# Three low bits of nine weight blocks taken from a byte on ScalarE; the order of the work searched anew

## The chip, the core and the metric

The kernel runs on one core of a Trainium2 chip. The metric is the device time of one execution, in microseconds (us); lower is better. The engines are TensorE (PE; its weight loads are shown apart as PEld), VectorE (DVE), ScalarE (ACT), GpSimd (POOL) and SyncE (SP), which issues nearly all DMAs.

## What is computed

Attention in which a query sees only the keys of its own cluster, followed by a feed-forward layer with a clipped square as its activation. Cut to what matters:

```python
# q, k, v: (4, 8, 768, 64) float32; centroids: (8, 16, 64)
q_assign = argmax(q_n . c_n); k_assign = argmax(k_n . c_n)      # normed rows
scores = where(q_assign == k_assign, q @ k.T / 8, -1e9)
attn = softmax(scores) @ v
x = attn laid out as (3072, 512)
h = x @ w_in                     # w_in: (512, 2048), w_out: (2048, 512)
g = where(h >= 1, h, where(h <= -1, 0, (h + 1)**2 / 4))
out = g @ w_out
```

The two weight matrices come in as float64. The kernel reads each weight as two 32-bit words, a low and a high one, and builds the float32 of it by shifting bits.

## The kernel before

The 3072 tokens are worked in twelve units u of 256 tokens, three to a batch entry. A unit has four pairs of heads, and a pair has four score tiles of 128 x 768. For each tile TensorE makes the scores into a two-bank PSUM buffer `pair` (`at_scores`), VectorE evicts them with their row minimum into `sS` (the instruction shown as CUSTOM_DVE_ANT_0, called an eviction below; evictions are counted from 1, so the 17th is the first of the second unit), ScalarE takes the exponential (`at_soft`), and TensorE multiplies with v (`at_av`). The first unit works in float32 and transposes its exponentials on TensorE; later units split each number into two float16 parts, which ScalarE and GpSimd make, and transpose by DMA. Then each unit goes through eight blocks f of 256 hidden columns (`ffn1`, `ffn2`).

Ahead of the first score tile stand the loads of q and k, their scaling and splitting, the labels (`labels`: products with the centroids and five VectorE passes that find the nearest one) and the mask rows made of the labels (`k_assign`, `q_pairs`). `v_bound` finds the largest v of a pair of heads (one VectorE reduction each, tile `v_am`).

Beside this the weights are prepared once, in sixteen blocks i = 2f + a (a is 0 for w_in, 1 for w_out), each of 1024 numbers on 128 partitions. A block is loaded with two DMAs (`w_load`) and then goes through `w_bits` (L1152): ScalarE takes the absolute value of the high words, scaled, into `t` (the buffers o, wk in the profile); VectorE shifts `t` left by three (L1170, the shift pass); TensorE sums columns of `t` to bound the weights (`w_sum`); VectorE ORs in the top three bits of the low words (the OR pass); and VectorE ORs in the sign while it writes the finished block to `w` (the sign pass). In the profile the shift pass is TENSOR_SCALAR 128x1024 and the other two are SCALAR_TENSOR_TENSOR 128x1024. `w_split` later makes the float16 parts.

What runs when is not the order of the code. Every operation goes to a `Recorder`, which holds the graph of what depends on what. `issue` runs a planner of its own forward and backward over it, `BASE` times, then shifts priorities by a list of numbers (`NUDGES`), each the seed of one change of priorities that `nudge` makes, and writes all instructions out in the order of the last forward pass. Each engine then takes its own instructions strictly in that order, and so does SP with the DMAs. Since all of them are written out by one helper, every row of the profile has line L376, and rows are told apart by their tiles.

Of the kernel before, what the change touches and what calls it, by code (L numbers as in the profile page):

```python
# [10 lines left out]
BF16 = mybir.dt.bfloat16  # L11
F32 = mybir.dt.float32
U32 = mybir.dt.uint32
AF = mybir.ActivationFunctionType
ALU = mybir.AluOpType
AX = mybir.AxisListType
# [26 lines left out]
FETCH = [128 * k - min(42, 4 + 9 * k) for k in range(1, 80)]  # L43

LOOK, MARGIN = 0.4, 4000
BASE = 21
NUDGES = (
# [29 lines left out]
)  # L77
TILED = 248

# [457 lines left out]
def tile_clustered_attention_moe(  # L537
# [38 lines left out]
    EARLY_SPLITS = 4  # L576
    WA, WR = -4, 2.6

    RAW = [3, 4, 5, 6, 7, 4, 5, 6, 0, 7, 6, 7, 0, 7, 0, None]
    rec = Recorder(tc)  # L580
    const = ctx.enter_context(tc.tile_pool(name="const", bufs=1))
# [195 lines left out]
    def k_scale(b, hp):  # L777
# [14 lines left out]

        ib = ar.bitcast(U32)
        rec.vector.tensor_scalar(
# [357 lines left out]
    def w_bits(a, f, part=None):  # L1152

        raw = WL.pop((a, f, part))
# [3 lines left out]
        t = WL[a, f][0][:, (part or 0) * 512 :][:, :n]  # L1158
        dst = w32[a][f][:, (part or 0) * 512 :][:, :n]
        tf = t.bitcast(F32)  # L1160
        if not w_wide:
# [5 lines left out]

        lo, hi = (raw.rearrange("p (f a) -> p f a", a=2)[:, :, x] for x in range(2))
        rec.scalar.activation(out=tf, in_=hi.bitcast(F32), func=AF.Abs, scale=2.0**-112)
        rec.vector.tensor_scalar(out=t, in0=t, scalar1=3, scalar2=None, op0=ALU.logical_shift_left)  # L1170
        w_sum(a, f, part)

# [2 lines left out]
            out=to, in0=lo, scalar=29, in1=t, op0=ALU.logical_shift_right, op1=ALU.bitwise_or  # L1175
        )
        rec.vector.scalar_tensor_tensor(
            out=dst, in0=hi, scalar=0x80000000, in1=to, op0=ALU.bitwise_and, op1=ALU.bitwise_or
# [192 lines left out]
    for i in range(2 * NF):  # L1371
        f, a = divmod(i, 2)
# [47 lines left out]
```

## Time and profile before

| | us |
|---|---|
| median of 3 runs | 852.74 (852.6 to 853.91) |
| the profiled execution | 851.57 |
| its span, from the first to the last instruction | 849.8 |
| PE busy | 808.7 (95%) |
| ACT busy | 657.6 (77%) |
| DVE busy | 633.3 (75%) |
| POOL busy | 529.5 (62%) |

The shares are means over the whole span. The kernel has a first part, in which loads, labels, float32 attention and weight preparation come together, and a long even part behind it, so the page's forty slices, and the busy time of each engine by stretch, say more than the means do. The rows themselves stand further below.

### The profile page before, as it was taken

How to read it: one execution, taken by the hardware profiler on the slowest of the kernel's cores; microseconds unless marked ns; L12 is line 12 of the kernel's file. 1: busy time of each engine (PE TensorE's matmuls, PEld its weight loads, DVE VectorE, ACT ScalarE, POOL GpSimd, SP SyncE). 2: the span in 40 equal slices, each digit the busy share in tenths (PEclk: the TensorE clock that was granted, in tenths of full speed). 3: DMA queues.
4: the chain of work that ended last, by engine and by line, in shares of the span. 5: the costliest groups of instructions: out<-in, count | busy, mean ns of one | idle time of the engine just before them, and what ended most of it. 6: DMA issues, size and time to landing. Idle time of an engine off the chain costs nothing.

```text
span 849.8 us, 18811 instructions
## 1 busy us (share of the span) xinstructions
PE 808.7 (95%) x7052; PEld 559.7 (66%) x7052; DVE 633.3 (75%) x1400; ACT 657.6 (77%) x1166; POOL 529.5 (62%) x510
## 2 busy tenths in 40 slices
PE   3686999999999999999999999999999999999998
PEld 2465776666766676766776767666676667677664
DVE  6999998999897768578888658677888766454322
ACT  6778999899987788788778688788778778676332
POOL 1121698978987568666767668657667668566222
PEclk9699999999999999999999999999999999999999
DMA  8967899979989779879989779889999788565100
GB/s 296 311 178 199 229 198 202 191 137 208 185 174 187 152 160 187 162 152 223 215 168 186 133 152 180 173 186 196 196 179 158 124 163 157 98 133 109 24 25 25
DMA packets 404763, 142.50 MB, mean 168 GB/s; under 512 B 372800, under 2 KB 396352, under 8 KB 404672
## 3 DMA queue, kind: packets, MB, share of 16 engines
q1 hardware_dynamic: 404672, 141.30, 82.0%
q8 instruction: 55, 0.90, 0.5%
q14 instruction: 36, 0.29, 0.1%
HBM read 40.40 MB, written 6.29 MB: 55 GB/s over the span
## 4 chain that ended last, share of the span: by engine, by line
PE 71%; DVE 7%; ACT 5%; issue 4%; POOL 3%; DMA 1%; POOLq 0%; DVEq 0%; ACTq 0%
PE pair L376 36%; PE banka L376 10%; PE banki L376 9%; PE bankh L376 9%; PE bankj L376 8%; DVE sS L376 2%; POOL hl L376 2%; DMA pT<-hl 1%; ACT hl L376 1%; ACT sS L376 1%; POOL w L376 1%; DVE r L376 1%; DVE w L376 1%; DVE bankh L376 1%; ACT w L376 1%
## 5 line engine op out<-in xcount | busy, mean ns | idle before, releaser
L376 POOL TENSOR_TENSOR hl<-sS,hl 128x768 f16<-128x768 f32 x176 | 297.6, 1694 | 113.5 <-ACT hl L376 96.9
L376 PE MATMUL pair<-w,g 128*128 128x512 f16 (+1 forms) x1120 | 277.3, 391 | 0.6 <-DVE w L376 0.6
L376 PEld LDWEIGHTS <-w 128*128 128x128 f16 x2112 | 204.8, 98 | 40.6 <-issue 1.6
L376 DVE CUSTOM_DVE_ANT_0 sS<-pair,zero,er 128x768 f32<-128x768 f32 x192 | 193.8, 1011 | 50.5 <-PE pair L376 41.2
L376 ACT ACTIVATE sS<-sS,sbi 128x768 f32<-128x768 f32 x192 | 179.1, 933 | 66.9 <-DVE sbi L376 61.7
L376 PEld LDWEIGHTS <-g 128*128 128x128 f16 x1056 | 101.6, 98 | 106.8 <-issue 1.2
L376 PE MATMUL pair<-kv,q 128*128 128x384 f16 x768 | 157.9, 329 | 6.9 <-DVE sbi L376 4.5
L376 ACT CAST hl<-sS 128x768 f16<-128x768 f32 x176 | 144.8, 826 | 7.3 <-DMA pT<-hl 5.4
L376 POOL TENSOR_TENSOR g<-r,g 128x512 f16<-128x512 f32 x80 | 95.4, 1192 | 75.5 <-ACT g L376 65.6
L376 PEld LDWEIGHTS <-q 128*128 128x128 f16 x992 | 78.3, 98 | 62.2 <-issue 18.5
L376 PE MATMUL banka<-pT,kv 128*64 128x256 f16 (+1 forms) x1680 | 104.8, 279 | 0.0
L376 PEld LDWEIGHTS <-kv 128*64 128x64 f16 (+1 forms) x1824 | 92.1, 108 | 5.5 <-DMA kv<-n 1.9
L376 ACT ACTIVATE r<-r,f_ra,f_rs 128x512 f32<-128x512 f32 x80 | 64.8, 810 | 38.3 <-DVE r L376 37.9
L376 POOL TENSOR_TENSOR qn<-qn,phi 128x256 f16<-128x256 f16 x48 | 32.7, 697 | 41.2 <-DVE phi L376 15.6
L376 PE MATMUL bankj<-x,w 128*128 128x256 f16 (+1 forms) x424 | 57.4, 289 | 0.0
L376 ACT CAST g<-r 128x512 f16<-128x512 f32 x80 | 48.7, 609 | 8.8 <-DVE r L376 5.5
L376 PE MATMUL bankh<-x,w 128*128 128x256 f16 (+1 forms) x376 | 47.2, 277 | 0.0
L376 PE MATMUL banki<-x,w 128*128 128x256 f16 (+1 forms) x288 | 39.9, 291 | 0.0
L376 PE MATMUL banki<-wk,w 128*128 128x256 f16 x312 | 37.0, 273 | 0.0
L376 ACT ACTIVATION_READ_ACCUMULATOR sS<-sS,sbi 128x1 f32 x192 | 36.0, 188 | 0.0
L376 DVE TENSOR_SCALAR r<-bankh,f_lo,f_hi 128x512 f32<-128x512 f32 x27 | 21.8, 808 | 18.2 <-PE bankh L376 16.3
L376 DVE TENSOR_SCALAR r<-banki,f_lo,f_hi 128x512 f32<-128x512 f32 x27 | 21.8, 808 | 15.9 <-PE banki L376 10.7
(262 smaller groups left out, 1108.5 us busy)
## 6 DMA issues: line engine op xcount, KB each, us to landing
w<-in_moe_w_out_dram SPq DMA_DIRECT2D x14, 512.0 KB, 6.0
kv<-in_k_dram SPq DMA_DIRECT2D x16, 384.0 KB, 3.9
q<-in_q_dram SPq DMA_DIRECT2D x12, 512.0 KB, 4.9
kv<-in_v_dram SPq DMA_DIRECT2D x16, 384.0 KB, 4.2
out_dram<-o SPq DMA_DIRECT2D x11, 512.0 KB, 3.4
w<-in_moe_w_in_dram SPq DMA_DIRECT2D x10, 512.0 KB, 5.3
word<-in_moe_w_in_dram SPq DMA_DIRECT2D x6, 512.0 KB, 4.8
o<-in_v_dram SPq DMA_DIRECT2D x8, 384.0 KB, 3.8
```

The lines of the kernel that those rows point to most:

```text
L376: fn(*args, **kw)
```

## The change

For the first nine blocks (i = 0 to 8) `w_bits` takes another way. The top byte of each low word is read as an unsigned byte, every eighth byte of the raw block. ScalarE computes byte/32 - 15.5/32 and writes it as an integer over the low word, which leaves the top three bits of the byte. VectorE then shifts `t` and ORs in these bits in one instruction, and the sign pass follows as before. So these blocks have two passes on ScalarE and two on VectorE, where there were one and three. `w_sum` now stands behind the pass that has the low bits in it. The other seven blocks stay as they were. `BASE` goes from 21 to 24, and the list of seeds is a new one.

```diff
+U8 = mybir.dt.uint8
...
-BASE = 21
+BASE = 24
 NUDGES = (
...
+    LO3 = range(9)
     RAW = [3, 4, 5, 6, 7, 4, 5, 6, 0, 7, 6, 7, 0, 7, 0, None]
...
         rec.scalar.activation(out=tf, in_=hi.bitcast(F32), func=AF.Abs, scale=2.0**-112)
+        if part is None and 2 * f + a in LO3:
+
+            top = raw.bitcast(U8).rearrange("p (f a) -> p f a", a=8)[:, :, 3]
+            rec.scalar.activation(out=lo, in_=top, func=AF.Copy, scale=2.0**-5, bias=-15.5 / 32)
+            rec.vector.scalar_tensor_tensor(
+                out=t, in0=t, scalar=3, in1=lo, op0=ALU.logical_shift_left, op1=ALU.bitwise_or
+            )
+            w_sum(a, f, part)
+            rec.vector.scalar_tensor_tensor(
+                out=dst, in0=hi, scalar=0x80000000, in1=t, op0=ALU.bitwise_and, op1=ALU.bitwise_or
+            )
+            return
         rec.vector.tensor_scalar(out=t, in0=t, scalar1=3, scalar2=None, op0=ALU.logical_shift_left)
```

Counted over the whole program, VectorE has 6 shift passes of 128x1024 where it had 15, ScalarE has 40 ACTIVATEs of 128x1024 where it had 31, and every other kind of instruction has its old count on every engine. Their order is new nearly everywhere. In the rows below, `qn` and `n` are the split q and k, `mx` the first label pass, and a trailing number tells buffers of one kind apart.

VectorE near the head of the program, from the first splits of q and k to the first label pass, before:

```order
L376 TENSOR_REDUCE v_am_155<-kv_61 128x1
L376 SCALAR_TENSOR_TENSOR qn_67<-q_65,sq_128,qn_67 128x4x64 x4
L376 SCALAR_TENSOR_TENSOR n_77<-kv_61,sc_135,n_77 128x12x64
L376 TENSOR_SCALAR o_68<-o_68 128x1024
L376 SCALAR_TENSOR_TENSOR w_78<-w_78,o_68 128x1024
L376 SCALAR_TENSOR_TENSOR w_78<-w_78 128x1024
L376 TENSOR_REDUCE mx_138<-bankj 128x16
```

and now:

```order
L384 RECIPROCAL sc_135<-ik_130 128x1
L384 SCALAR_TENSOR_TENSOR qn_67<-q_65,sq_128,qn_67 128x4x64 x4
L384 SCALAR_TENSOR_TENSOR n_77<-kv_61,sc_135,n_77 128x12x64
L384 TENSOR_REDUCE mx_138<-bankj 128x16
L384 TENSOR_TENSOR bankj<-bankj,mx_138 128x256
```

The reduction of v and the three passes of the first weight block have left the place between the splits and the labels; the block's two passes now follow the labels.

VectorE just ahead of the 17th eviction, before:

```order
L376 TENSOR_REDUCE w_am<-bankh 128x2
L376 SCALAR_TENSOR_TENSOR w_78<-w_78 128x1024
L376 TENSOR_SCALAR bankj<-w_am 128x8
L376 TENSOR_SCALAR wk_69<-wk_69 128x1024
L376 RECIPROCAL rs_151<-rs_151 128x4
L376 TENSOR_SCALAR w_iw<-bankj 128x8
L376 SCALAR_TENSOR_TENSOR hl_167<-kv_61,sv_164,hl_167 128x768
L376 RECIPROCAL w_sw<-w_iw 128x8
L376 SCALAR_TENSOR_TENSOR word_71<-word_71,wk_69 128x1024
L376 ISA sS_87,sbi_144<-pair_79,zero,er_140 128x768
```

and now:

```order
L384 TENSOR_REDUCE w_am<-bankh 128x2
L384 SCALAR_TENSOR_TENSOR hl_167<-kv_61,sv_164,hl_167 128x768
L384 SCALAR_TENSOR_TENSOR wk_69<-wk_69,word_71 128x1024
L384 TENSOR_SCALAR bankj<-w_am 128x8
L384 RECIPROCAL rs_151<-rs_151 128x4
L384 SCALAR_TENSOR_TENSOR w_78<-word_71,wk_69 128x1024
L384 TENSOR_SCALAR w_iw<-bankj 128x8
L384 ISA sS_87,sbi_144<-pair_79,zero,er_140 128x768
```

Ahead of this eviction VectorE had 10 shift passes and 18 OR and sign passes, and now has 1 and 20; four `v_am` reductions stand ahead of it in both. TensorE has exactly the same matmuls, kind by kind, ahead of the 17th score product in both programs, and again ahead of the 49th. ScalarE has 12 ACTIVATEs of 128x1024 ahead of the 17th exponential before, and 20 now.

ScalarE between the copies of the first transposes (`q`, `kv` from `pair`) and the copies of the mask rows, before:

```order
L376 COPY kv_61<-pair_80 128x768 x2
L376 ACTIVATE x_73,am_133<-kv_63 128x768
L376 ACTIVATE wk_69<-w_78 128x1024
L376 ACTIVATE n_77<-kv_62,sc_136 128x12x64
L376 ACTIVATE q_65<-q_65,phi_141 128x512
L376 COPY kv_61<-pair_79 128x768 x2
```

and now:

```order
L384 COPY kv_61<-pair_80 128x768 x2
L384 ACTIVATE o_68<-w_78 128x1024
L384 ACTIVATE w_78<-w_78 128x1024
L384 ACTIVATE x_73,am_133<-kv_63 128x768
L384 ACTIVATE wk_69<-w_78 128x1024
L384 ACTIVATE w_78<-w_78 128x1024
L384 ACTIVATE q_65<-q_65,phi_141 128x512
L384 COPY q_65<-pair_80 128x256 x2
L384 COPY kv_61<-pair_79 128x768
```

Two weight blocks with both their passes (w_78 written from w_78 is the new pass) now stand there in place of one block's single pass.

## Rows read from the trace of the kernel before

**Rows 1.** The page, parts 1 and 2: busy us with the share of the span and the instructions; then the span in 40 equal slices of 21.2 us, in tenths.

```profile
PE 808.7 (95%) x7052; PEld 559.7 (66%) x7052; DVE 633.3 (75%) x1400; ACT 657.6 (77%) x1166; POOL 529.5 (62%) x510
...
PE   3686999999999999999999999999999999999998
...
DVE  6999998999897768578888658677888766454322
ACT  6778999899987788788778688788778778676332
...
PEclk9699999999999999999999999999999999999999
```

**Rows 2.** Busy time by stretch: the stretch and its length, then busy us (and instructions) of PE, PEld, DVE, ACT and POOL, the granted TensorE clock as a share of 2.4 GHz, the DMA share and GB/s.

```profile
10.00:88.00 78.00, 56.10 (x569) 41.14 (x569) 75.50 (x188) 60.30 (x100) 13.28 (x20) 0.85 0.88 245
88.00:250.00 162.00, 156.80 (x1214) 107.49 (x1213) 146.97 (x285) 150.36 (x253) 132.45 (x98) 1.00 0.91 188
250.00:840.00 590.00, 589.76 (x5246) 408.46 (x5245) 405.73 (x913) 440.29 (x804) 380.63 (x366) 1.00 0.81 152
840.00:849.80 9.80, 5.71 (x27) 2.39 (x25) 1.46 (x3) 1.56 (x3) 1.15 (x1) 0.92 0.14 54
```

**Rows 3.** Waits of VectorE in the first 88 us, whom it waited for: us in total, times, longest. All but the last three fall before 8 us.

```profile
DVE sS L376 <- DMA sS<-in_centroids_dram: 4.5, 1, 4.5
DVE aq L376 <- DMA q<-in_q_dram: 1.2, 1, 1.2
DVE c_rn L376 <- ACT c_nrm L376: 0.6, 1, 0.6
DVE x L376 <- ACT x L376: 0.6, 1, 0.6
DVE sS L376 <- PE pair L376: 0.2, 1, 0.2
DVE banki L376 <- PE banki L376: 0.2, 1, 0.2
```

**Rows 4.** VectorE by kind of instruction from 10 to 88 us: out<-in, shapes and count, then busy us and mean ns of one, then idle time ahead. First the shift passes, then the OR and sign passes.

```profile
L376 DVE TENSOR_SCALAR o<-o 128x1024 uint32<-128x1024 uint32 x5 | 3.4, 686 | 0.1
L376 DVE TENSOR_SCALAR wk<-wk 128x1024 uint32<-128x1024 uint32 x5 | 3.4, 682 | 0.0
...
L376 DVE SCALAR_TENSOR_TENSOR w<-w 128x1024 uint32<-128x1024 uint32 x8 | 10.1, 1268 | 0.0
L376 DVE SCALAR_TENSOR_TENSOR w<-w,o 128x1024 uint32<-128x1024 uint32 x5 | 6.1, 1225 | 0.0
L376 DVE SCALAR_TENSOR_TENSOR w<-w,wk 128x1024 uint32<-128x1024 uint32 x4 | 4.9, 1216 | 0.0
```

**Rows 5.** VectorE in order of time: start, duration, instruction. Each pair is a weight pass and the instruction behind it; the difference of the two starts is what the pass takes of VectorE's time.

```profile
26.61 1.22 DVE L376 SCALAR_TENSOR_TENSOR w<-w,wk 128x1024 uint32<-128x1024 uint32 x1
27.75 0.16 DVE L376 RECIPROCAL phi<-banki 128x1 f32<-128x1 f32 x1
...
43.18 0.68 DVE L376 TENSOR_SCALAR wk<-wk 128x1024 uint32<-128x1024 uint32 x1
43.78 1.01 DVE L376 CUSTOM_DVE_ANT_0 sS<-pair,zero,er 128x768 f32<-128x768 f32 x1
```

**Rows 6.** ScalarE in the same way: a weight block's first pass, which reads every second word, and a cast of 128x1024 that reads its input densely, each with the instruction behind it.

```profile
26.99 1.16 ACT L376 ACTIVATE o<-w 128x1024 f32<-128x1024 f32 x1 [1.80 <-DMA w<-in_moe_w_out_dram]
28.05 0.63 ACT L376 COPY q<-pair 128x256 bf16<-128x256 bf16 x2
...
113.83 1.06 ACT L376 CAST w<-wk 128x1024 f16<-128x1024 f32 x1
114.77 0.66 ACT L376 ACTIVATE g<-g 128x512 f32<-128x512 f32 x1
```

**Rows 7.** The longest waits of ScalarE from 10 to 88 us, in the form of rows 3.

```profile
ACT sS L376 <- DVE sbi L376: 5.7, 6, 1.9
ACT n L376 <- DVE sc L376: 2.6, 1, 2.6
ACT pT L376 <- PE pair L376: 2.3, 4, 0.9
ACT o L376 <- DMA w<-in_moe_w_out_dram: 1.8, 1, 1.8
ACT wk L376 <- DMA w<-in_moe_w_in_dram: 1.3, 1, 1.3
```

**Rows 8.** VectorE in order of time at the head (the first reduction of v; the shift pass of the first block; the first label pass) and at the 17th eviction.

```profile
9.33 0.92 DVE L376 TENSOR_REDUCE v_am<-kv 128x1 bf16<-128x768 f32 x1
10.25 1.68 DVE L376 SCALAR_TENSOR_TENSOR qn<-q,sq,qn 128x256 f16<-128x256 f32 x4
...
12.78 0.69 DVE L376 TENSOR_SCALAR o<-o 128x1024 uint32<-128x1024 uint32 x1
...
16.08 0.42 DVE L376 TENSOR_REDUCE mx<-bankj 128x16 f32<-128x256 f32 x1
...
87.82 1.02 DVE L376 CUSTOM_DVE_ANT_0 sS<-pair,zero,er 128x768 f32<-128x768 f32 x1 [0.20 <-PE pair L376]
```

**Rows 9.** All waits of TensorE from 85 to 250 us, in the form of rows 3; `sbi` is the row minimum that an eviction writes.

```profile
PE pair L376 <- DVE sbi L376: 4.5, 6, 1.1
PE pair L376 <- DVE w L376: 0.6, 1, 0.6
```

65 rows, old and new, of the table NUDGES are left out of this document.

## The prediction

> **What bounds the kernel now.** I read the page's slices first, then busy time by stretch, then who waited for whom in the stretches that are not full. The slices [rows 1] show TensorE below nine tenths only in the first four (some 85 us) and in the last one. The stretches [rows 2] put sizes to it. From 250 to 840 us TensorE is busy for 589.76 of 590 us: nothing that another engine saves there can shorten the run. From 88 to 250 us it is busy for 156.8 of 162 us, so 5.2 us are idle. From 10 to 88 us it is busy for 56.1 of 78 us, and there VectorE is busy for 75.5 of 78. VectorE's own waits say the same more sharply [rows 3]: behind the first 8 us it waited three times in 80 us, for 0.6 + 0.2 + 0.2 = 1.0 us together. So up to the 17th eviction at 87.82 us [rows 8] the kernel lives on VectorE's time, behind it on TensorE's, and a saving counts as far as it brings the point forward at which TensorE becomes full, or takes away some of the 5.2 us of idle time behind that point. ScalarE is not free beside it: 60.3 of 78 us busy from 10 to 88, and 150.4 of 162 behind it [rows 2].
>
> **What the edit takes off VectorE.** A shift pass lasts 0.68 us by itself but holds VectorE for 0.60 (43.78 - 43.18), since instructions overlap [rows 5]. Ten of them ran between 10 and 88 us [rows 4], the nine that fall away among them. 9 x 0.60 = 5.4 us. The pass that now shifts and ORs has the operands of the old OR pass, t and the strided low words; that one held VectorE for 1.14 us (27.75 - 26.61) [rows 5], the sign pass is unchanged, and so I price both at 1.14 as before. A bound for the OR with a shift on the other operand is the mean of the sign passes, 1.27 against 1.22 us [rows 4]: 0.05 more in each of nine, 0.5 us in all, and nothing below.
>
> **What it puts on ScalarE.** Nine passes of 1024 elements. No row shows ScalarE reading bytes or writing every second word. The nearest is the block's first pass, which reads every second word and holds ScalarE for 1.06 us (28.05 - 26.99); a dense cast of that length takes 0.94 (114.77 - 113.83) [rows 6]. If the strided write costs as much again as the strided read does, it is 1.18. I take 1.06, nearest to the first: 9.5 us in all, with 8.5 and 10.6 as ends. I cost this at nothing, because ScalarE's idle time from 10 to 88 us is 78 - 60.3 = 17.7 us [rows 2], nearly twice that. If that cover is gone the whole 9.5 us would stand in the chain; that is the second rival below.
>
> The Trainium skill (ScalarE: Activation LUTs, section Rules for kernel authors) speaks against such a move: it gives adding, multiplying and the like to VectorE, as the faster engine for each element. The rows agree on the price, 0.60 against 1.06 us, so by that rule the edit loses 9 x 0.46 = 4.1 us of engine time. It would be right if the two engines were equally full; which of them is empty decides, and rows 2 say ScalarE.
>
> **The wait that it adds.** VectorE's first pass of a block now waits for two ScalarE passes, 1.06 us more. Behind it on VectorE wait whatever stands next, at the head the scaling of the second k, later evictions; and TensorE's `w_sum` waits for a pass of 1.14 us where it waited for one of 0.60. The new order sets both ScalarE passes several instructions ahead of the VectorE pass (at the head, before the second k's exponent and the copies of the mask rows), so I cost it at 0, with 0.3 us for each of nine, 2.7 us, as the other end: that is about what one of the three late VectorE waits cost now [rows 3].
>
> **What the new order does up to the 17th eviction.** TensorE has the same matmuls ahead of it in both programs, so this is a fair mark. VectorE has 9 shift passes fewer and 2 OR and sign passes more ahead of it: -5.4 + 2 x 1.14 = -3.1 us of work. But not all of it is time. Before, the gap between the splits and the first label pass was filled: 0.9 us of reduction of v (10.25 - 9.33) and 3.3 us of the first weight block (16.08 - 12.78) [rows 8], 4.2 us together. Now nothing stands in that gap, and the labels still need the transposes, ScalarE's copies and the products first. VectorE idles there, less what the labels' chain gains by no longer standing behind that work. Ends: 0 and 4.2 us of new idle time. I take 2.5, above the middle, since ScalarE's copies and TensorE's transposes were not behind VectorE's fill work but beside it. So the 17th eviction comes 3.1 - 2.5 = 0.6 us sooner, with ends of 3.1 sooner and 1.1 later.
>
> **What it does behind.** At the 49th score product TensorE again has the same matmuls ahead of it in both, and by then all sixteen blocks are done in both. So VectorE has its full 5.4 us less, minus 2.5 idle at the head: it stands 2.9 us better, TensorE only 0.6 us. The difference, 2.3 us, is slack that TensorE's waits can use up. It waited for evictions 6 times here, 4.5 us in all and never over 1.1 [rows 9]. With 2.3 us of slack all six could go; but the order beside each is another, and ScalarE, 93% busy there (150.36 of 162) [rows 2], feeds the same buffers. I take away 2.6 of the 4.5, with 0 and 4.5 as ends. GpSimd and the DMA queue keep their counts; their new order adds nothing that these rows price.
>
> **The sum** against the profiled execution of 851.57 us: -0.6 (head) - 2.6 (behind) = -3.2, which is 848.4. The median of the runs is 852.74, 1.2 above that execution, so on the median's scale 849.5. TensorE's clock is not in the sum: it was granted 0.85 of full speed from 10 to 88 us and 1.00 behind [rows 2], and in the first stretch TensorE is not the bound. About 0.2%, 1.7 us, is what a measurement of this kernel can tell from no change.
>
> **Rivals.**
>
> *More comes through.* VectorE finds work at the head after all (idle 0) and all waits for evictions go: -3.1 - 4.5 = -7.6, 845.1; half of that way beyond the forecast is 847. For it: VectorE's waits are nearly none now [rows 3], so a planner that keeps it full is at hand. Against: the empty gap between splits and labels.
>
> *ScalarE takes the place of VectorE, and it is slower.* The place is 10 to 88 us. Ahead of the 17th exponential ScalarE has 20 passes of 1024 where it had 12, 8 x 1.06 = 8.5 us more. Its idle time is 17.7 us, but most of that is waiting for others: 5.7 us for evictions, 2.6 for a scale, 2.3 for transposes, 3.1 for weights to land [rows 7]. Passes can fill a wait only if their block has landed and the engine is not needed again just then. The point that decides: if more than 17.7 - 8.5 = 9.2 us of the idle time stay, the 17th exponential comes later than now. If 13 us stay, it is 3.8 us later, TensorE fills up as much later, and the time is 856.5. For it: in the head two blocks with four ScalarE passes now stand ahead of the copies of the mask rows. Against: 17.7 us is twice 8.5.
>
> *No difference.* The head's new idle time takes all 3.1 us, and behind 88 us the waits for evictions turn into waits for something else, since three engines are over 90% busy there [rows 2]: 852.7, within 1.7.
>
> That the change does not do what it says is excluded: the counted passes go from 15 to 6 on VectorE and from 31 to 40 on ScalarE.
>
> **How the numbers follow.** Forecast, 1.7 to 5 us faster: 0.46. More, 5 to 8 us faster: 0.13. No difference: 0.25. Slower through ScalarE: 0.16. So faster 0.59, same 0.25, slower 0.16. For the range I leave out the far half of the first rival and most of the slower one beyond the edge of no difference: 846.0 to 854.5. The forecast's own part of it is 847.7 to 851.0.
>
> **What would show it.** In the changed profile: TensorE's idle time between 10 and 88 us within 1 us of the 21.9 us now, and its idle time from 88 to 250 us near 2.6 instead of 5.2; VectorE idle for some 2 to 3 us just ahead of the first label pass; the 17th eviction at some 87.2 us; ScalarE near 68 of 78 us busy from 10 to 88, with the new pass at 1.1 to 1.2 us by itself. I am wrong if the 17th eviction is later than 88 us with VectorE waiting for ScalarE, if the new pass lasts clearly over 1.3 us, or if TensorE has idle time behind 250 us, which the sum leaves out.

## The result, and the profile after

The changed kernel is slower: 855.38 us, median of 7 runs (854.32 to 856.55), against 851.25 (850.32 to 853.91, 7 runs) for the kernel before beside it. The ratio is 1.0054 with a 95% interval of 1.0042 to 1.0066. The prediction of 849.5 us, 3.2 us faster, was wrong in sign. The profiled execution spans 853.3 us and took 855.38; helper lines now read L384.

The page of the changed kernel, parts 1 and 2 as in [rows 1]:

```profile
PE 809.5 (95%) x7052; PEld 558.1 (65%) x7052; DVE 630.7 (74%) x1391; ACT 666.4 (78%) x1175; POOL 528.2 (62%) x510
...
PE   3678999999999999999999999999999999999998
...
PEclk9799999999999999999999999999999999999999
```

The edit itself is all there: nine instructions fewer on VectorE and 2.6 us less busy, nine more on ScalarE and 8.8 us more. (Nine shift passes of 0.68 us are 6.1 us, so VectorE's other work, the same in count, lasts some 3.5 us longer in the new order.) TensorE has the same matmuls and is busy 0.8 us longer, so with a span 3.5 us longer it idles 2.7 us more. Busy time by stretch, as in [rows 2], says where:

```profile
10.00:88.00 78.00, 55.52 (x568) 38.96 (x566) 71.01 (x176) 66.07 (x106) 12.79 (x19) 0.91 0.89 252
88.00:250.00 162.00, 155.49 (x1199) 106.30 (x1200) 145.23 (x283) 149.31 (x251) 129.50 (x99) 1.00 0.90 186
250.00:840.00 590.00, 587.76 (x5228) 406.87 (x5227) 406.03 (x912) 440.97 (x804) 381.64 (x365) 1.00 0.81 152
```

TensorE's idle time is 78 - 55.52 = 22.5 us in the first stretch (21.9 before), 6.5 in the second (5.2 before) and 2.2 in the third (0.2 before). VectorE, 75.5 of 78 us busy before, is now busy for 71.0. Of the difference 1.5 us have moved ahead of 10 us; the other 3.0, near the 3.1 us of work that the prediction counted, have become idle time. Its three longest waits between 8 and 90 us, in the form of [rows 3], and its order of time at the head and at the 17th eviction, as [rows 8]:

```profile
DVE mx L384 <- PE bankj L384: 3.6, 2, 2.4
DVE sS L384 <- PE pair L384: 1.1, 3, 0.7
DVE n L384 <- ACT n L384: 1.0, 2, 0.7
```

```profile
10.29 1.02 DVE L384 SCALAR_TENSOR_TENSOR n<-kv,sc,n 128x768 f16<-128x768 f32 x1 [0.34 <-ACT n L384]
13.70 0.42 DVE L384 TENSOR_REDUCE mx<-bankj 128x16 f32<-128x256 f32 x1 [2.40 <-PE bankj L384]
...
87.90 1.02 DVE L384 CUSTOM_DVE_ANT_0 sS<-pair,zero,er 128x768 f32<-128x768 f32 x1
```

The 2.40 us of idle time stand just ahead of the first label pass. The first eviction comes at 24.60 us where it came at 30.35, but the 5th at 42.69 where it came at 42.19, and the 17th at 87.90 where it came at 87.82: the lead is gone early. What has grown in TensorE's waits from 10 to 90 us are those for ScalarE's exponentials (`sS`) and for its copies of the transposes (`pT`), now and then before:

```profile
PE pair L384 <- ACT sS L384: 9.2, 8, 1.6
PE pair L384 <- ACT pT L384: 5.7, 8, 1.5
```

```profile
PE pair L376 <- ACT sS L376: 6.7, 6, 2.5
PE pair L376 <- ACT pT L376: 1.6, 4, 0.6
```

They are 14.9 us where they were 8.3, while those for VectorE's splits (`qn`, `n`) fell from 9.4 to 4.2. Part of them is VectorE again, because the exponentials themselves waited 6.7 us for evictions. The new passes, by kind and then two in order of time, as [rows 4] and [rows 6]:

```profile
L384 ACT ACTIVATE w<-w 128x1024 uint32<-128x1024 uint8 x8 | 9.1, 1134 | 0.0
```

```profile
L384 DVE SCALAR_TENSOR_TENSOR o<-o,w 128x1024 uint32<-128x1024 uint32 x4 | 4.9, 1220 | 0.0
L384 DVE SCALAR_TENSOR_TENSOR wk<-wk,w 128x1024 uint32<-128x1024 uint32 x4 | 4.9, 1217 | 0.0
...
```

```profile
18.68 1.15 ACT L384 ACTIVATE w<-w 128x1024 uint32<-128x1024 uint8 x1
19.72 0.71 ACT L384 ACTIVATE q<-q,phi 128x512 f16<-128x512 f16 x1
```

The byte pass holds ScalarE for 19.72 - 18.68 = 1.04 us and the shift+OR lasts as long as the old OR. Last, the five longest groups of waits of TensorE behind 88 us up to 840, in the form of [rows 9]:

```profile
PE pair L384 <- DVE sbi L384: 3.9, 3, 1.8
PE bankj L384 <- DVE r L384: 1.3, 2, 1.1
PE banka L384 <- DMA pT<-hl: 1.2, 1, 1.2
PE bankh L384 <- DVE has L384: 0.9, 1, 0.9
PE banki L384 <- DVE r L384: 0.5, 1, 0.5
```

Six waits for evictions have become three longer ones, and there are waits of kinds that the kernel before had none of: for VectorE's pass on r, for a transposing DMA (at 388 us) and for `has` (at 400 us). The last two lie 300 us behind the nine blocks. So the first theory was **A: the order that came with the edit costs the time**; the rival **B: the edit itself costs it, ScalarE's passes standing ahead of evictions in the head**.

### The profile page after: what moved, and what is told of

Its sections match the earlier page's. It is cut to its first block, busy times and chain, and to the rows that moved or that the text cites. A ratio compares the mean times of both kernels' runs of the same rounds, so it can differ in the third digit from the quotient of the medians.

```text
span 853.3 us, 18822 instructions
## 1 busy us (share of the span) xinstructions
PE 809.5 (95%) x7052; PEld 558.1 (65%) x7052; DVE 630.7 (74%) x1391; ACT 666.4 (78%) x1175; POOL 528.2 (62%) x510
## 4 chain that ended last, share of the span: by engine, by line
PE 80%; DVE 9%; ACT 4%; DMA 3%; issue 3%; POOL 0%; SPq 0%; DVEq 0%; ACTq 0%; POOLq 0%
PE pair L384 40%; PE banka L384 11%; PE banki L384 10%; PE bankj L384 9%; PE bankh L384 9%; DVE sS L384 3%; DMA pT<-hl 1%; DVE r L384 1%; DMA kv<-n 1%; ACT hl L384 1%; DVE w L384 1%; ACT w L384 1%; ACT sS L384 1%; DMA w<-in_moe_w_out_dram 1%; DMA q<-in_q_dram 1%
## 5 line engine op out<-in xcount | busy, mean ns | idle before, releaser
L384 POOL TENSOR_TENSOR hl<-sS,hl 128x768 f16<-128x768 f32 x176 | 297.3, 1692 | 111.7 <-ACT hl L384 86.2
L384 PE MATMUL pair<-w,g 128*128 128x512 f16 (+1 forms) x1120 | 278.4, 391 | 0.1
L384 DVE CUSTOM_DVE_ANT_0 sS<-pair,zero,er 128x768 f32<-128x768 f32 x192 | 194.3, 1012 | 63.2 <-PE pair L384 48.2
L384 PEld LDWEIGHTS <-w 128*128 128x128 f16 x2112 | 204.7, 98 | 43.7 <-issue 5.1
L384 ACT ACTIVATE sS<-sS,sbi 128x768 f32<-128x768 f32 x192 | 178.9, 932 | 65.9 <-DVE sbi L384 57.9
L384 PEld LDWEIGHTS <-g 128*128 128x128 f16 x1056 | 100.9, 98 | 104.1 <-issue 2.2
L384 PE MATMUL pair<-kv,q 128*128 128x384 f16 x768 | 159.1, 331 | 9.7 <-ACT pT L384 5.7
L384 ACT CAST hl<-sS 128x768 f16<-128x768 f32 x176 | 145.1, 826 | 3.6 <-DMA pT<-hl 1.4
L384 POOL TENSOR_TENSOR g<-r,g 128x512 f16<-128x512 f32 x80 | 97.1, 1213 | 67.8 <-ACT g L384 62.8
L384 PEld LDWEIGHTS <-q 128*128 128x128 f16 x992 | 79.9, 98 | 65.1 <-issue 22.0
L384 PE MATMUL banka<-pT,kv 128*64 128x256 f16 (+1 forms) x1680 | 105.3, 279 | 1.2 <-DMA pT<-hl 1.2
L384 PEld LDWEIGHTS <-kv 128*64 128x64 f16 (+1 forms) x1824 | 92.6, 109 | 6.8 <-DMA kv<-n 2.3
L384 ACT ACTIVATE r<-r,f_ra,f_rs 128x512 f32<-128x512 f32 x80 | 64.8, 810 | 35.6 <-DVE r L384 35.2
L384 PE MATMUL bankj<-x,w 128*128 128x256 f16 (+1 forms) x424 | 58.1, 289 | 1.4 <-DVE r L384 1.3
L384 ACT CAST g<-r 128x512 f16<-128x512 f32 x80 | 48.7, 609 | 13.1 <-DVE r L384 9.2
L384 POOL TENSOR_TENSOR qn<-qn,phi 128x256 f16<-128x256 f16 x48 | 32.7, 694 | 36.9 <-DVE phi L384 27.2
L384 PE MATMUL bankh<-x,w 128*128 128x256 f16 (+1 forms) x376 | 46.5, 277 | 0.0
L384 PE MATMUL banki<-x,w 128*128 128x256 f16 (+1 forms) x288 | 40.4, 291 | 0.8 <-DVE r L384 0.5
L384 PE MATMUL banki<-wk,w 128*128 128x256 f16 x312 | 37.5, 273 | 0.0
L384 ACT ACTIVATE q<-q,phi 128x512 f16<-128x512 f16 x48 | 33.5, 714 | 4.8 <-PE bankh L384 3.0
L384 ACT ACTIVATION_READ_ACCUMULATOR sS<-sS,sbi 128x1 f32 x192 | 36.0, 188 | 0.0
L384 DVE TENSOR_SCALAR r<-banki,f_lo,f_hi 128x512 f32<-128x512 f32 x27 | 21.8, 809 | 16.6 <-PE banki L384 13.4
```

The costliest lines, as they stand in the source:

```text
L384: fn(*args, **kw)
```

## The experiments

All times in one table; the edits below it are shown shortened. The ratio is to the kernel before on the same chip. "17th" is the start of the 17th eviction; the last two columns are TensorE's idle time from 88 to 250 and from 250 to 835 us, length less busy time in the profile of the run.

| run | passes, order | us (runs) | ratio, 95% | 17th | 88-250 | 250-835 |
|---|---|---|---|---|---|---|
| before | old, old | 850.5 to 851.3 | 1 | 87.82 | 5.2 | 0.2 |
| after | new, new | 855.38 (7) | 1.0042-1.0066 | 87.90 | 6.5 | 2.2 |
| e1 | new, old | 857.15 (6) | 1.0052-1.0083 | 93.66 | 5.5 | 0.6 |
| e2 | old, new | 859.09 (5) | 1.0078-1.0103 | 91.92 | 6.3 | 1.8 |
| e3 | new, new mended | 857.36 (6) | 1.0059-1.0090 | 87.69 | 6.1 | 3.9 |
| e4 | new, old | 855.05 (6) | 1.0032-1.0064 | 94.29 | 4.7 | 0.6 |
| e5 | old, unsearched | 865.68 (4) | 1.0155-1.0192 | 91.16 | 7.9 | 7.0 |
| e6 | new, unsearched | 862.84 (4) | 1.0122-1.0159 | 89.81 | 5.5 | 7.1 |
| e7 | new, new mended | 853.44 (9) | 1.0014-1.0042 | 87.04 | 6.4 | 0.7 |
| e8 | new, new mended more | 853.65 (12) | 1.0024-1.0048 | 86.86 | 6.2 | 1.1 |
| e9 | new less byte pass, new | 854.00 (8) | 1.0024-1.0050 | 86.35 | 6.4 | 1.7 |
| e10 | new less byte pass, old | 850.93 (12) | 0.9981-1.0008 | 88.46 | 4.0 | 0.1 |
| d1 | new, fresh a | 855.15 (4) | 1.0030-1.0065 | 85.09 | 5.4 | 4.0 |
| d2 | new, fresh b | 857.18 (4) | 1.0060-1.0097 | 91.98 | 4.6 | 2.9 |
| b1 | old, fresh a' | 851.17 (10) | 0.9992-1.0019 | 85.00 | 2.5 | 3.1 |
| b2 | old, fresh b' | 855.71 (4) | 1.0036-1.0079 | 87.45 | 5.7 | 5.0 |
| d3 | new less byte pass, fresh a | 856.73 (7) | 1.0028-1.0071 | 84.72 | 6.0 | 5.8 |
| b3 | new, fresh a' | 854.52 (6) | 1.0028-1.0053 | 87.70 | 2.6 | 2.6 |
| d4 | new, c | 854.28 (8) | 1.0025-1.0058 | 89.50 | 3.7 | 1.8 |
| b4 | old, c' | 853.57 (10) | 1.0019-1.0043 | 85.16 | 5.7 | 1.7 |

**e1 and e4: the edit in the old order.** In e1 each new pass takes an old one's place; in e4 the sign pass stands where the OR stood.

```diff
 rec.scalar.activation(out=tf, in_=hi.bitcast(F32), func=AF.Abs, ...)
+n_abs.calls.append((nc.scalar.activation, (), dict(out=lo, in_=top, func=AF.Copy, ...)))
+n_shift.calls[:] = [(nc.vector.scalar_tensor_tensor, (), dict(out=t, in0=t, scalar=3, in1=lo, ...))]
-n_or.calls[:] = []              # e1
+n_or.calls[:] = n_sign.calls    # e4, with n_sign.calls = [] and in1=t
```

> The new passes of the nine weight blocks put into the order of the kernel before: the byte pass stands on ScalarE right behind the block's Abs, the shift+OR pass stands where the shift stood, the OR pass falls away and the sign pass reads the other half. Every TensorE instruction stands where it stood in the kernel before. Theory A (the new order costs the time, the edit itself is neutral or a small gain): within 0.3% of the kernel before, 847 to 852.5 us on the scale where that one is 851.3; TensorE's idle time behind 250 us stays at the 0.2 us of the kernel before and the wait at 388 us is not there. Theory B (the edit costs it: ScalarE's nine passes take VectorE's place in the head, and what follows is late): 3 to 5 us slower than the kernel before, 854 to 856 us, with the 17th eviction later than 88 us or TensorE's waits for ScalarE's sS and pT longer by some 5 us.

> The edit in the order of the kernel before again, with one change against the first of these: the new sign pass stands where the old OR pass stood, instead of where the old sign pass stood, so that the half-done block is read before ScalarE's next Abs writes over it (in the first the next block's passes came in between, so that VectorE and ScalarE waited for one another there in a way that neither kernel has, and nine blocks held other bits). Theory A (the order costs the time, the edit is neutral or a small gain): within 0.3% of the kernel before, 848 to 852.5 us where that one has 851.0; the 5.8 us that the first one lost ahead of 91 us were its false waits. Theory B (the edit costs it: ScalarE's passes stand ahead of evictions of TensorE's products): still 3 to 6 us slower, 854 to 857 us, with TensorE's waits for ScalarE's sS ahead of 95 us near the 10.7 us of the first (6.7 us in the kernel before).

A fell for this order: the edit alone costs it 4.3 us (855.05 - 850.79), and the loss is made ahead of the 17th eviction, which comes 6.5 us later (94.29); behind 250 us almost no idle time is added. In e1 nine blocks hold other bits than they should, for the reason that the expectation of e4 gives. Its median lies above both of its expectations, but its profile spans 855.2 us and that of e4 855.1 (the medians are 2.1 us apart, with intervals that overlap), so its waits were not false ones, as had been expected of it. TensorE's waits for ScalarE's sS up to 95 us are 11.5 us in e4 where they were 6.7, as B said. TensorE's clock was granted at 1.00 (2.4 GHz) from 10 to 87 us, so it has no part in the 5.0 us by which the 15th and the 16th eviction come later. It has one in the last 1.5 us: behind a wait of 3.20 us it was granted 0.50 (1.2 GHz) from 90 to 94 us, and the 17th and 18th score products took 2.74 us there, 1.61 in the kernel before. The timeline of e4, ScalarE and then TensorE:

```profile
75.49 1.13 ACT L377 ACTIVATE w<-w 128x1024 uint32<-128x1024 uint8 x1
76.50 0.81 ACT L377 ACTIVATE pT<-pair 128x768 f32<-128x768 f32 x1
```

```profile
77.36 0.81 PE L377 MATMUL pair<-kv,q 128*128 128x384 f16 x4 [1.55 <-ACT pT L377]
```

The copy of the transposes out of `pair` starts when the byte pass lets go of ScalarE, and TensorE waits for that copy. ScalarE's idle time from 10 to 88 us (78 - 63.9 = 14.1 us) is no cover, because it stands elsewhere.

**e2: the old passes in the new order.**

```diff
+n_lo.calls[:] = []
+n_shift.calls[:] = [(nc.vector.tensor_scalar, (), dict(out=t, in0=t, scalar1=3, ...))]
+n_sign.calls[:0] = [(nc.vector.scalar_tensor_tensor, (), dict(out=lo, in0=lo, scalar=29, in1=t, ...))]
```

> The order of the changed kernel with the old passes: ScalarE's byte pass is left out, VectorE's shift stands where the shift+OR stands, and the OR pass (1.14 us) comes back right ahead of the sign pass. Theory A (order): as slow as the changed kernel or slower by up to 5 us (VectorE has nine passes more in an order that leaves no place for them), 855 to 860 us where the kernel before has 851.3; the waits near 388 and 400 us are still there. Theory B (the edit): back at the kernel before, 850 to 852.5 us.

Here the edit is worth the other sign: without it the new order takes 859.09 us, 3.7 more than with it, and the 17th eviction comes 4.0 us later. So the edit costs 4.3 us in the one order and gives 3.7 in the other.

**e9 and e10: ScalarE's part taken out**, in the new and in the old order.

```diff
-activation(out=lo, in_=top, func=AF.Copy, ...)
+activation(out=lo[:, :1], in_=top[:, :1], func=AF.Copy, ...)
-scalar_tensor_tensor(out=t, in0=t, scalar=3, in1=lo, ...)
+scalar_tensor_tensor(out=t, in0=t, scalar=3, in1=lo[:, :1].to_broadcast([P, 1024]), ...)
```

The pass handles one column of 1024, and the low bits of all columns are taken from it.

> The changed kernel with ScalarE's byte pass cut to one column of 1024 (about 0.2 us in place of 1.13), which the shift+OR reads in all columns: ScalarE's work of the edit is left out, VectorE's is as in the changed kernel (the low bits are those of one column). If ScalarE's idle time covers the passes in the new order, as the prediction had it: within 0.5 us of the changed kernel, and the 17th eviction within 0.5 us of 87.9. If the passes hold up evictions on ScalarE in the head: 2 to 5 us faster than the changed kernel, 850.5 to 853.5 us, with the 17th eviction at 84 to 86 us and TensorE's waits for ScalarE's sS and pT down from 14.9 us to some 9.

> The same cut of ScalarE's byte pass, in the order of the kernel before (the second of the runs with the edit in that order, 855.1 us, with the pass cut to one column). If the 4.3 us that the edit costs there are ScalarE's nine passes ahead of its evictions: 3.5 to 7 us faster than that run, 848 to 851.5 us, that is, at or under the kernel before (850.8), since VectorE's nine shorter block chains are then all that is left. If they come from VectorE's changed passes (a sign pass that comes earlier, a shift+OR that waits): still 854 to 856 us.

In the old order the byte passes are 4.1 us (855.05 - 850.93), nearly the whole loss. In the new order they are 1.4 (855.38 - 854.00), which lies between the two expectations and which the intervals do not tell from none; TensorE's waits for `sS` and `pT` fell only from 14.9 to 13.3 us, and the 17th eviction comes 1.6 us sooner. The sharper result is e10 beside the kernel before. VectorE has its nine passes less and the order is the old one, yet the time is the same and the 17th eviction no sooner. Busy time of e10 from 10 to 88 us, and the wait of VectorE that has grown most (in [rows 3] it was 0.2 us):

```profile
10.00:88.00 78.00, 56.14 (x565) 40.33 (x566) 71.99 (x179) 60.22 (x108) 13.84 (x20) 0.83 0.89 247
```

```profile
DVE sS L377 <- PE pair L377: 3.2, 5, 1.3
```

VectorE is busy 3.5 us less there (71.99 against 75.50) and waits 3.0 us more for score products. Followed one by one, its evictions win time and lose it again: beside the kernel before the 1st comes 0.9 us sooner, the 6th 0.5 later, the 12th 1.1 sooner, the 15th level and the 17th 0.6 later. At two of these places it is the order of VectorE's own passes: what falls away here is the last pass of a block, and the first one has grown. Ahead of the 6th eviction the shift+OR holds VectorE for 1.13 us (43.10 to 44.23) where the shift held it for 0.60 [rows 5]. Ahead of the 15th it is the same, and there VectorE does not wait once from the 14th eviction on (73.53 to 81.23), so it still sets the pace. Ahead of the 17th it is TensorE; e10, then the kernel before:

```profile
83.35 2.82 PE L377 MATMUL pair<-idf,sS 128*128 128x128 f32 x12 [3.00 <-ACT sS L377]
...
86.83 2.76 PE L377 MATMUL pair<-kv,q 128*128 128x384 f16 x8
```

```profile
83.39 2.68 PE L376 MATMUL pair<-idf,sS 128*128 128x128 f32 x12 [2.47 <-ACT sS L376]
...
86.72 1.61 PE L376 MATMUL pair<-kv,q 128*128 128x384 f16 x8
```

Behind these waits both have a granted clock of 0.50 (1.2 GHz) from 85 to 87 us; from 87 to 90 it is 1.00 in the kernel before and 0.59 in e10, whose 17th and 18th products (the last line of each) take 1.15 us longer. So e10 shows that 3.5 us less of VectorE's work are worth nothing in this order. It does not show that VectorE sets no pace there, and no run tells what the nine passes are worth in the old order if the shorter block stood otherwise.

**e3, e7 and e8: local mends of the new order.** e3 and e7 change the order around the two late products at 388 and 400 us; e8 adds four moves on VectorE that put an eviction, or the pass on r, ahead of the pass that had held it up. `ahead(i, j)` puts operation i ahead of j, `behind(i, j)` puts it behind j, with what depends on it.

```diff
 self.forward(prio)
+self.behind(1785, 1812), self.behind(1840, 1835)                                                # e3
+self.ahead(1801, 1785), self.ahead(1812, 1785), self.ahead(1802, 1787), self.behind(1840, 1835)  # e7
+self.ahead(539, 594), self.behind(570, 582), self.behind(702, 839), self.ahead(946, 957)         # e8, with e7's
```

> The changed kernel with two local moves 300 us behind the edited blocks: the product of the gathered attention that waited 1.20 us at 388 us for its transposing DMA goes behind three products that are ready (two of 4 and 6 matmuls and the 12 of a pooling product), and on VectorE the pass on r that stood ahead of `has` (0.80 us, TensorE waited 0.87 us) goes behind it. Theory A: 1 to 2.5 us faster than the changed kernel, 852.9 to 854.4 us where that one has 855.4 and the kernel before 851.3, and TensorE's idle time from 376 to 404 us falls from 2.07 us to under 1. Theory B (the loss is made in the head and only shows later): the waits return elsewhere and the time stays within 0.5 us of the changed kernel.

> The changed kernel with another mend of the two waits at 388 and 400 us. The first mend put the gathered attention's product behind the pooling product, which itself waits for a transposing DMA until 389.3 us, and lost 1.7 us. Here only the score product (4 matmuls) and one output product (6 matmuls, 1.3 us), which are both ready, go ahead of it, with the eviction of the score product ahead of the VectorE pass that waits for the gathered attention; the pooling product stays behind; `has` goes ahead of the pass on r, as before. If the 2.5 us at 385 to 400 us are the local order: TensorE's idle time from 376 to 404 us falls from 2.07 us to under 1 and the time by 1 to 2 us against the changed kernel, to 853.3 to 854.4 us. If the queue of transposing DMAs is what is late there, whatever TensorE does: the wait moves to the pooling product, and nothing is won (854.9 to 855.9 us).

> The changed kernel with the mends of the run before (853.4 us) and four more on VectorE, whose order alone changes: at 121, 134 and 180 us an eviction of a score product goes ahead of a long pass that ran 1.0 to 2.7 us while TensorE waited for the eviction (1.78, 1.14 and 1.02 us), and at 202 us the pass on r goes ahead of a small pass that took 1.65 us (TensorE waited 1.12 us). If the order is what the changed kernel loses by behind 100 us: these waits of 5.1 us shrink to under 1.5 us, TensorE's idle time from 88 to 250 us falls from 6.4 to 3 us or less, and the time comes down by 2 to 4 us, to 849.5 to 851.5 us, level with the kernel before (850.8) or just under it. If the waits are only moved on (each engine is full there, and what is put behind is late next): TensorE's idle time stays within 1 us of 6.4 and the time at 853 to 854 us.

e7 took 1.9 us off (855.38 to 853.44) and TensorE's idle time behind 250 us fell from 2.2 to 0.7: those waits were the order's alone. e3, slower than either of its expectations, had put the product behind another that waits for its own transposing DMA, and its idle time there rose to 3.9 us. e8 took all four of its waits away and won nothing: idle time from 88 to 250 us stayed at 6.2. TensorE's waits of e8 at the places that took over, and what VectorE and GpSimd did ahead of the second:

```profile
132.85 1.99 PE L384 MATMUL banki<-x,w 128*128 128x256 f32 x8 [1.43 <-DVE w_am L384]
...
146.94 0.81 PE L384 MATMUL pair<-kv,q 128*128 128x384 f16 x4 [2.92 <-DVE sbi L384]
```

```profile
142.89 3.06 DVE L384 SCALAR_TENSOR_TENSOR w<-w,o 128x1024 uint32<-128x1024 uint32 x1
145.87 1.00 DVE L384 CUSTOM_DVE_ANT_0 sS<-pair,zero,er 128x768 f32<-128x768 f32 x1
```

```profile
142.70 2.17 POOL L384 TENSOR_TENSOR w<-wk,w 128x1024 f16<-128x1024 f32 x1
144.83 2.62 POOL L384 TENSOR_TENSOR hl<-sS,hl 128x768 f16<-128x768 f32 x1
```

The sign pass, 1.2 us elsewhere [rows 4], took 3.06 and ended 1.1 us behind GpSimd's running instruction (144.87). The eviction stood behind it, and TensorE behind the eviction.

**e5 and e6: both kernels without their seeds.**

```diff
-for seed in NUDGES:
+for seed in NUDGES[:0]:
```

> The kernel before with its planner's order as it comes out of the 21 sweeps, with none of its 257 seeded changes of priority. Theory A (places of the order set the time by microseconds, whatever the edit): 5 to 12 us slower than the kernel before, 856 to 863 us, spread over waits at single places of the whole span. Theory B (the order matters little behind the head, the passes decide): within 2 us of the kernel before.

> The changed kernel with its planner's order as it comes out of the 24 sweeps, with none of its 318 seeded changes of priority; to be set against the kernel before without its seeds. Theory A: slower than the changed kernel by 3 to 10 us (858 to 865 us), and not slower than the kernel before without its seeds: the edit gives 2 to 4 us there, as it does in the changed kernel's order (857.1 us of span with the old passes, 853.3 with the new). Theory B: slower than the kernel before without its seeds by 3 us or more, as the changed kernel is slower than the kernel before.

Unsearched, the changed kernel is 2.8 us ahead (862.84 against 865.68), but it comes from 24 sweeps and the other from 21, so this is not the edit alone. e5 is slower than either of its expectations. The search took 14.9 us off the kernel before but only 7.5 off the changed one.

**Fresh orders.** For three pairs the search by the planner's own estimate was made again, equally long for both sets of passes: from 24 sweeps (d1, b1), from 21 sweeps (d2, b2), and on behind each kernel's own seeds (d4, b4). Only the numbers in NUDGES, and BASE for the sweeps, differ. b3 puts the new passes into b1's order as in e4; d3 is d1 with the byte pass cut as in e9.

> The edit as it is, in a fresh order: 24 sweeps of the planner, then seeds searched anew by the planner's own estimate until it is no higher than for the changed kernel's order. If what an order is worth on the chip is open by a few us among orders that the planner holds equal: this run and the next lie 2 us or more apart from each other or from the changed kernel (855.4), somewhere between 849 and 859 us. If the edit itself costs 4 us whatever the order: both within 1.5 us of 855.

> The edit in a second fresh order, from 21 sweeps, searched in the same way. Expectations as for the first; and if the edit is worth 2 to 4 us once the order is free, the mean of the two lies that much under the mean of the two orders of the old passes that run beside them; if VectorE's saved passes are used up by ScalarE's added ones, the two means are within 2 us.

> The kernel before with a fresh order, from 24 sweeps, searched in the same way and as long. If the order that the kernel before has is a lucky one on the chip: slower than it by 2 to 6 us (853 to 857 us where it has 850.6). If the planner's estimate carries over: within 1.5 us of it.

> The kernel before with a second fresh order, from 21 sweeps, searched in the same way. Expectations as for the first of these two.

> The first fresh order with the edit (855.2 us), with ScalarE's byte pass cut to one column of 1024 as before (its work is left out). If the price of the byte pass is set by the order: between the 1.4 us of the changed kernel's order and the 4.1 us of the old one, 851 to 854 us. If a good order hides it: within 0.7 us of 855.2.

> The first fresh order of the old passes (851.2 us), with the new passes put into the old places, as in the second run with the edit in the old order. If an order that was searched with one set of passes always pays for the other: 853.5 to 857 us, as the old order did (plus 4.3 us). If the plus 4.3 us was a matter of that order alone: within 1.5 us of 851.2.

> The changed kernel with its own seeds and the search carried on behind them, by the planner's estimate: the third pair, with the next run. If the edit costs time in a searched order too: above the next run by 1.5 to 5 us, 853 to 857 us.

> The kernel before with its own seeds and the search carried on behind them; the planner holds this order the best of all. If its estimate carries over by a microsecond: 847.5 to 850 us, faster than both kernels. If orders that it holds near each other lie up to 5 us apart on the chip: anything from 848 to 856.

These orders carry some 8,000 to 8,800 seeds, the two kernels themselves 257 and 318, so those two come from another search. With them there are four orders of each: old passes 850.8, 851.2, 855.7 and 853.6 (mean 852.8), new passes 855.4, 855.2, 857.2 and 854.3 (mean 855.5). By pairs of ratios the edit costs 0.54, 0.43, 0.22 and 0.10%, 0.32% or 2.7 us in the mean. The four scatter by 0.20%, so the 95% interval of their mean is about plus or minus 0.32%: it reaches down to about zero. The three fresh pairs alone give 0.25%, plus or minus 0.41. Orders of one set of passes lie up to 4.9 us apart, and b1 and b2, searched alike, 4.5. The planner's own estimate does not carry over by a microsecond either: b4, which it held the best of all, takes 853.57 us, where 847.5 to 850 would have shown that it does; d4 lies only 0.7 us above it. b3 costs 3.4 us against b1, as e4 did against the kernel before. d3 gained nothing on d1, against both of its expectations: its 17th eviction comes 0.4 us sooner, and TensorE's idle time behind 250 us is 1.8 us longer. Busy time from 250 to 835 us, of the kernel before, d1 and b2:

```profile
250.00:835.00 585.00, 584.76 (x5210) 404.93 (x5209) 403.10 (x909) 438.05 (x801) 379.48 (x365) 1.00 0.81 153
```

```profile
250.00:835.00 585.00, 581.00 (x5147) 400.63 (x5146) 403.73 (x905) 437.42 (x795) 375.83 (x361) 1.00 0.81 152
```

```profile
250.00:835.00 585.00, 579.97 (x5171) 401.30 (x5169) 405.31 (x912) 439.51 (x801) 376.73 (x363) 1.00 0.82 154
```

TensorE has 0.24 us idle there in the old order and 1.7 to 5.0 in each of the six that were searched again, with either set of passes; in d1 that is more than the 2.7 us by which its 17th eviction comes sooner. That the old order has none is what is peculiar to it. No version beat the kernel before.

## Why the prediction was wrong, step by step

The span grew by 3.5 us where the sum said 3.2 less. Of these 6.7 us, nearly all is found: 0.7 lie in the head's term, 3.9 in the term for 88 to 250 us and 2.0 behind 250 us, for which the sum had no term. The last two are the steps that failed in the changed kernel; the first hides a wrong step that came out right.

- **The prices** held: the shift+OR at 1.22 us by itself (priced like the old OR), the byte pass at 1.13 by itself and 1.04 from start to start (priced 1.06). What VectorE saves held in the old order, where its busy time over the span fell by 5.9 us (e10), but not in the new one, where it fell by 2.6.
- **The head** held in its parts: 2.40 us of idle time ahead of the first label pass (2.5 taken), the 17th eviction at 87.90 us (87.2 forecast, ends 84.7 and 88.9), a term of +0.1 for -0.6.
- **"The kernel lives on VectorE's time" up to the 17th eviction** led to adding up the lengths of its passes as time of the kernel, and that failed in the old order. e10 takes 3.5 us of work off VectorE in that stretch, and the 17th eviction does not move forward (88.46). What counted was which pass stood ahead of an eviction, and at the last one TensorE. In the new order the same passes are worth 5.1 us (859.09 for e2, 854.00 for e9), near the 5.4 forecast. That the head's term came out near its forecast belongs to the new order, and rows of the old one could not show it: this part was luck.
- **"I cost this at nothing"**, the byte passes under 17.7 us of ScalarE's idle time, failed in the old order (4.1 us, e4 against e10), was 1.4 or none in the new one (e9), and none to be seen in d1's (d3). The second rival's mechanism is real: e4 shows TensorE behind a byte pass. It was given 0.16 and its size, 3.8 us, was about right in the old order; in the changed kernel it is at most a part.
- **"I take away 2.6 of the 4.5"** behind 88 us is the term that was furthest off: idle time from 88 to 250 us rose by 1.3, so it missed by 3.9 us. VectorE was busy 1.7 us less there (145.23 against 146.97), but that took no waits off TensorE, because the waits belong to the order. The prediction said that "the order beside each is another" and still kept them as the ones to be taken from. e8 shows why neither sign could be read from the old rows: four waits removed came back as others.
- **"Anything behind 250 us", left out of the sum**, came to 2.0 us of new idle time. The prediction had seen that TensorE is full there and cannot gain, but a new order can lose there. It was named as what would make the prediction wrong. e7 shows that 1.5 of it was two places of the order.

Together: +0.1 to the 17th eviction, +1.3 up to 250 us and +2.0 behind is 3.4 of the 3.5 us by which the span grew. By cause it does not add up to one sum, because the parts depend on one another. By the way of e2 and e9, the order costs 8.1 us (859.09 - 851.03), VectorE's part gives 5.1 and ScalarE's costs 1.4. By the way of e10 and e4, VectorE's part gives nothing, ScalarE's costs 4.1 and the order 0.3. What stays open is whether some order makes the edit pay: in the four that were searched for it, it did not. That GpSimd's place in time is what moved the waits in e8 is argued from its timeline; no run took GpSimd's instructions away.

## What to carry over

When the order of many in-order engines is planned around the work, work taken off an engine near full counts only as far as it stood ahead of what others wait for: take it off alone, in the old order, before crediting it, and follow the marks on the way one by one, since a mean over the stretch hides where the time is won and lost. Price a pass moved to an emptier engine by what stands behind it in that engine's queue, not by the engine's idle share. And where an edit comes with a new order, run the edit in the old order, the old work in the new one, and a few fresh orders of both: here orders alone differ by up to 4.9 us, more than the edit.

## What the runs showed of the hardware

ScalarE reads bytes at a stride of 8 and writes every second 32-bit word of 1024 at 1.04 us from start to start, no slower than the block's first pass, which reads every second word (1.06) [rows 6].

VectorE's passes with two tensors in SBUF stretch beside GpSimd. In the changed kernel the OR of a later block, on VectorE and then with GpSimd beside it:

```profile
122.52 2.67 DVE L384 SCALAR_TENSOR_TENSOR word<-word,wk 128x1024 uint32<-128x1024 uint32 x1
125.11 1.01 DVE L384 CUSTOM_DVE_ANT_0 sS<-pair,zero,er 128x768 f32<-128x768 f32 x1
```

```profile
122.28 1.81 POOL L384 TENSOR_TENSOR hl<-sS,hl 128x768 f16<-128x768 f32 x1 [1.96 <-ACT hl L384]
124.06 3.11 POOL L384 TENSOR_TENSOR w<-wk,w 128x1024 f16<-128x1024 f32 x1
```

The pass ended at 125.19, 1.1 us behind the end of the first GpSimd instruction (124.09), and the second, 2.17 us in e8's row of its kind, took 3.11 and ended 2.0 us behind VectorE's pass. The eviction behind it came late and TensorE waited 1.77 us for it at 126.17. The Trainium skill (SBUF — State Buffer, section SBUF: two separate sides) states that VectorE, with two inputs in SBUF, and GpSimd take a shared port pair as an exclusive lock for a whole instruction. By that rule each waits for the other in turn, and this timeline agrees.
